# Casting the values of later batches on GpSimd, and loading half of w_in in smaller pieces

## The chip, the cores and the metric

The kernel runs on one core of one Trainium2 chip. The metric is the device time of one execution in microseconds (us); of several runs the median counts. A core has five engines that work side by side, each through its own queue in order: TensorE (PE in the profile, its weight loads PEld), VectorE (DVE), ScalarE (ACT), GpSimd (POOL) and SyncE (SP, which only issues transfers here). They wait for one another, and for transfers, through semaphores.

## What is computed

A linear attention with position-dependent features, and behind it a two-layer network. Per batch and head, for q, k, v of 576 rows and 64 columns:

```python
def phi(x, c, s):                       # c, s: cosine and sine of the row's position
    r = np.maximum(x, 0.0)
    return np.concatenate([r * c, r * s], axis=-1)
q_p, k_p = phi(q, cos_w, sin_w), phi(k, cos_w, sin_w)
kv = np.einsum('bhsf,bhsd->bhfd', k_p, v)
z = np.sum(k_p, axis=2)
num = np.einsum('bhsf,bhfd->bhsd', q_p, kv)
den = np.einsum('bhsf,bhf->bhs', q_p, z)[..., None] + 1e-06
x = num / den                           # 8 batches, 8 heads, then laid out as 4608 x 512
h = x @ w_in                            # 512 x 2048
g = np.maximum(h, 0.0) ** 2
out = g @ w_out                         # 2048 x 512
```

Inputs and output are fp32; the matmuls work on bf16.

## The kernel before

**The work of a batch.** The kernel goes through the 8 batches in turn. The 576 rows of a batch are four main tiles of 128 (j = 0 to 3) and a tail of 64 rows; for the tail, two groups of four heads lie above one another on the 128 partitions. For each batch:
- k, v and q are loaded as fp32 (`declare_load`): one main transfer of 1 MB and two of 64 KB for the tail each. Batch 0 is loaded at the start, batches 1 and 2 from POOL's queue, batches 3 to 7 from SP's queue. There is one buffer for each of k, v, q, so a load waits until the batch before has been read.
- Features (`declare_feature`, helper `relu_scale`, L406 on ACT and L408 on DVE): relu times cosine, relu times sine, to bf16.
- Values (`declare_v`): v is cast to bf16 into the tile vx, with a column of ones beside each head's 64 columns, so that the sums z come out of the same matmul. It has 65 columns a head, five main buffers and two for tails. From batch 3 on, all five casts of a batch are put on ACT (L413, helper `copy`).
- Key-value products (`declare_kz`): matmuls of kp and vx over the five tiles; then the numerators and denominators (`declare_num`), the division on DVE (L637 to L639), and a transpose of x. From batch 2 on the transposes of the query features and of x are DMAs from SP's queue.
- First layer: for batches 0 to 2 plain matmuls (`declare_plain`) with relu on ACT (L416) and square on DVE (L419); from batch 3 on a scheme with seven products instead of eight (`declare_seven1`), with sums of x and of w_in made on DVE (L427, tiles xs and w1s), added to a PSUM bank with relu by L422 on DVE.
- Second layer: `declare_rows` for batch 0, then `declare_pair`, again seven products, with sums of g (tile gs, L427) and results (ysb).

All matmuls of these stages go through the helper `mm`, L430.

**How the order is made.** The functions named `declare_...` don't issue anything. Each adds operations to a `Planner`, with the engines that may do it, an assumed cost, and what it reads and writes. The planner then plays the whole program through with these costs, picks an engine and a place in its queue for each operation, with hand-made shifts of due times (`SHIFTS`), and the kernel issues the operations in that order. So what stands ahead of what on an engine is fixed when the program is built; at run time an engine only waits. In `declare_v` the cost of a cast is 0.52 us on ACT and 0.34 on DVE for a main tile; `declare_att` calls it with ACT alone from batch 3 on.

**How w_in comes in.** `prologue` issues the loads of batch 0 from SP's queue. On POOL's queue it waits for the tail of v (L1090), and then issues w_in in four quarters of columns with `load_w1(i, 4)`, L373. A quarter is 512 columns for 512 rows: 128 partitions with four rows each, read as fp32 and written as bf16 (so the transfer casts). The planner is told of them by four entries that are `GIVEN`, one a quarter, 2.6 us apart. The first layer of batch 0 starts with columns 0 to 255 (blocks hb 0 and 1 of 128), then 256 to 511, and so on. POOL's later transfers (batches 1 and 2, w_out with `load_w2`, the output of batch 0) are in the plan; after some 56 us POOL has nothing more to do.

Of the kernel before, what the change touches and what calls it, by code (L numbers as in the profile page):

```python
# [10 lines left out]
ALU = mybir.AluOpType  # L11
# [40 lines left out]
class Planner:  # L52
# [23 lines left out]
    def add(self, engs, fn, r=(), w=(), pos=None, lat=None, size=None, after=(), land=2.2, held=None, begin=0.0):  # L76
        if isinstance(engs, tuple):
            engs = {engs[0]: engs[1]}
        if size:
            lat = land + size  # L80
        op = Op(engs, fn, pos, lat, size)
        op.land, op.held, op.begin = land, held, begin
        for k in r:
            if k in self.writer:
                op.deps.add(self.writer[k])
            self.readers.setdefault(k, []).append(op)
        for k in w:
            if k in self.writer:
                op.deps.add(self.writer[k])
            op.deps.update(x for x in self.readers.get(k, ()) if x is not op)  # L90
            self.writer[k], self.readers[k] = op, []
        for k in list(r) + list(w):
            b = k[0] if isinstance(k, tuple) else k
            if isinstance(b, Buf) and b not in op.bufs:
                op.bufs.append(b)
                b.users += 1
        op.after = set(after) - op.deps
        op.deps |= op.after
        self.ops.append(op)
        return op  # L100
# [133 lines left out]
def kernel(  # L234
# [9 lines left out]
    nc = tc.nc  # L244
    P = nc.NUM_PARTITIONS
    B, H, S, D = q.shape
# [70 lines left out]
    def at(buf, name=None):  # L317
        return mem[name or buf.pool][:, buf.i]
# [13 lines left out]
    def constants():  # L332
        sidx = const.tile([P, J + 1], F32, name="sidx")
        for p0, p1, c, n, base, mult in [
            (0, P, 0, J, 0, J),
            (0, TAIL, J, 1, MAIN, 1),
            (TAIL, P, J, 1, MAIN, 1),
        ]:
            nc.gpsimd.iota(
                sidx[p0:p1, c : c + n],  # L340
                pattern=[[1, n]],
                base=base,
                channel_multiplier=mult,
                allow_small_or_imprecise_dtypes=True,
            )
        bias_pi2 = const.tile([P, 1], F32, name="bias_pi2")
        nc.vector.memset(bias_pi2, math.pi / 2.0)
        theta_scale = (math.pi / 2.0) / S
        nc.scalar.activation(cos_col, sidx, ACTF.Sin, bias=bias_pi2[:], scale=-theta_scale)
        nc.scalar.activation(sin_col, sidx, ACTF.Sin, bias=0.0, scale=theta_scale)  # L350
        make_identity(nc, ident)
# [3 lines left out]
    def load_main(src, nm, i, b, eng, parts=(slice(None),)):  # L355
        main = mem[nm][:, i]
        for js in parts:
            eng.dma_start(  # L358
                out=main[:, :, js, :],
                in_=src[b, :, 0:MAIN, :].rearrange("h (p j) d -> p h j d", j=J)[:, :, js, :],  # L360
            )

    def load_tail(src, nm, i, b, eng):
        tail = mem[nm + "t"][:, i]
        for g in range(2):
            eng.dma_start(  # L366
                out=tail[g * TAIL : (g + 1) * TAIL, :, :],
                in_=src[b, g * HH : (g + 1) * HH, MAIN:S, :].rearrange("h p d -> p h d"),
            )

    def load_w1(i, n):
        f0, f1 = i * DFF // n, (i + 1) * DFF // n
        nc.gpsimd.dma_start(  # L373
            out=w1sb[:, :, f0:f1],
            in_=moe_w_in[:, f0:f1].rearrange("(kb p) f -> p kb f", p=P),
        )
# [35 lines left out]
    def copy(eng, out, in_):  # L412
        (nc.scalar.copy if eng == "ACT" else nc.vector.tensor_copy)(out=out, in_=in_)  # L413
# [39 lines left out]
    def cached(d, key, pool):  # L453
        if key not in d:
            d[key] = plan.buf(pool)
        return d[key]
# [15 lines left out]
    def source(nm, b, j):  # L472
        return loaded[nm if j < J else nm + "t", b]
# [6 lines left out]
    def piece(nm, b, j):  # L480
        t = at(source(nm, b, j))
        return t[:, :, j, :] if j < J else t
# [35 lines left out]
        add({e: cost[e] for e in engs}, feature, r=[source_key(nm, b, j)], w=[(buf, j % 2, part)])  # L518

    def declare_v(b, j, engs):  # L520
        buf = cached(vxb, (b, j), "vx" if j < J else "vxt")
        n = 1 if j < J else 0.65
        cost = {"ACT": 0.52 * n, "DVE": 0.34 * n}

        def cast(eng):
            copy(eng, at(buf)[:, :, 0:D], piece("v", b, j))

        add({e: cost[e] for e in engs}, cast, r=[source("v", b, j)], w=[buf])

# [501 lines left out]
    def declare_att(b, kpos, npos, cos_k=BOTH, cos_q=DVE1, cast=ACT1):  # L1031
        for j in range(NS):
            declare_feature("k", b, j, "c", cos_k)
            declare_feature("k", b, j, "s", ACT1)
            declare_v(b, j, cast)
        declare_kz(b, kpos)
        for j in range(NS):
            declare_feature("q", b, j, "c", cos_q)
            declare_feature("q", b, j, "s", ACT1)
            if b > 1 and (j == J or j % 2):  # L1040
                declare_qT(b, j // 2)
            elif b == 1:
                declare_qT_pe(b, j, npos[j] - 3.5, DVE1)
        for j in range(NS):
            declare_num(b, j, npos[j])
            if b > 1 and (j == J or j % 2):
                declare_xT(b, j // 2)
            elif b == 1:
                declare_xT_pe(b, j, npos[j] + 2.0, BOTH)
# [19 lines left out]
    def prologue():  # L1069
        for src, nm, part in (  # L1070
            (k, "k", 0), (k, "kt", 0), (q, "q", 0), (v, "vt", 0), (v, "v", 0), (v, "v", 1), (q, "q", 1), (q, "qt", 0)
        ):
            if nm[1:]:
                load_tail(src, nm[0], 0, 0, nc.sync)
            elif nm == "k":
                load_main(src, nm, 0, 0, nc.sync)
            elif nm == "q":
                load_main(src, nm, 0, 0, nc.sync, [slice(part * J // 2, (part + 1) * J // 2)])
            else:
                h = slice(part * HH, (part + 1) * HH)  # L1080
                nc.sync.dma_start(
                    out=mem["v"][:, 0, h],
                    in_=v[0, h, 0:MAIN, :].rearrange("h (p j) d -> p h j d", j=J),
                )
        nc.vector.memset(zeros, 0.0)
        for t in ("vx", "vxt"):
            nc.vector.memset(mem[t][:, :, :, D:E1], 1.0)
        constants()
        fill(28)
        nc.gpsimd.tensor_copy(out=w1sb[0:1, 0, 0:1], in_=mem["vt"][0:1, 0, 0, 0:1])  # L1090
        for i in range(4):
            load_w1(i, 4)

    def fill(n):
        for _ in range(n):
            nc.tensor.matmul(out=banks[:, SPARE, :], lhsT=zeros[:, 0:P], rhs=zeros, start=True, stop=True)
# [11 lines left out]
    def declare_first():  # L1108
# [4 lines left out]
        for j in range(2):  # L1113
            for c in "cs":
                feature("q", j, c)
        declare_v(0, J, BOTH)
        ks = [plan.buf("B"), plan.buf("B")]
        kvzb[0] = plan.buf("kvz")
# [185 lines left out]
    with tc.manual_schedule():  # L1304
        prologue()
        end = None
        for op in plan.plan(t0):
            if op.eng == "PE" and op.start < SPARE_UNTIL:
                if end:
                    fill(int((op.start - end - 0.2) / 0.22))  # L1310
                end = op.end
            op.fn(op.eng)
# [29 lines left out]
```

## Time and profile before

| what | value |
|---|---|
| median of 3 runs | 278.38 us (277.17 to 278.71) |
| the profiled execution | 276.82 us, span of its instructions 274.8 us |
| granted TensorE clock | 1.000 |
| matmuls and weight loads | 2845 each |
| DMA queue of POOL | 12.32 MB, 17.1% of 16 engines' span |
| DMA queue of SP and ACT | 40.12 MB, 58.4% |
| ACT casts of vx from v | 26 main ones, mean 636 ns |
| transfers of w_in | 4, median 10.5 us from issue to landing |

The profile shows one execution. Busy time is the time in which an engine has an instruction in work; matmuls are pipelined, so their durations overlap, and a short stop of PE shows in the distance from one start to the next rather than in its busy time. A group of instructions is given by line, engine, operation, the tiles out<-in, their shapes (partitions x elements, type) and their number; then busy time and the mean of one in ns, then the engine's idle time before them and what ended it. In a timeline each row is a start, a duration, and in brackets the idle time before it with what ended that. The chain of work that ended last is followed back from the last instruction to whatever released it.

### The profile page before, as it was taken

The page shows a single profiled execution, that of the slowest core. Times are in us where ns is not written, and L with a number is a line of the kernel's source. Part 1 is how long each engine was busy: PE and PEld are TensorE (multiplying, and loading weights), DVE is VectorE, ACT ScalarE, POOL GpSimd, SP SyncE. Part 2 cuts the span into 40 slices and gives each one's busy share as a digit, 9 for nine tenths or more (in the row PEclk, how much of TensorE's full clock was granted, in tenths as well). Part 3 has the DMA queues.
Part 4 walks back from the last instruction along what each step waited for, and adds up shares of the span by engine and source line. Part 5 has one row for each costly group of instructions (what it writes and reads, how often), then busy time and mean ns, then how long its engine had stood idle before and what let it go on. Part 6 is the DMA issues. An engine that isn't in the chain of part 4 may idle for free.

```text
span 274.8 us, 7115 instructions
## 1 busy us (share of the span) xinstructions
PE 267.9 (98%) x2845; PEld 227.6 (83%) x2845; DVE 218.9 (80%) x515; ACT 194.9 (71%) x391; POOL 21.6 (8%) x38
## 2 busy tenths in 40 slices
PE   8979999999999999999999999999999999999994
PEld 3668856789988988888888898988988888888884
DVE  1789996997694989699968999799968798279652
ACT  3876982997895598589957994699735954684522
POOL 1453544010000000000000000000000000000000
PEclk9999999999999999999999999999999999999999
DMA  7999999969979998899299955996198301200025
GB/s 217 321 205 290 296 283 365 219 218 225 361 160 186 281 334 156 224 347 221 81 164 308 259 181 102 265 338 217 35 205 170 91 2 44 95 16 2 1 79 153
DMA packets 81840, 53.01 MB, mean 193 GB/s; under 512 B 53584, under 2 KB 77648, under 8 KB 81808
## 3 DMA queue, kind: packets, MB, share of 16 engines
q1 hardware_dynamic: 75136, 40.12, 58.4%
q0 software_dynamic: 6528, 12.32, 17.1%
q8 instruction: 22, 0.36, 0.5%
q10 hardware_dynamic: 144, 0.13, 0.1%
q14 instruction: 10, 0.08, 0.1%
HBM read 36.70 MB, written 9.44 MB: 168 GB/s over the span
## 4 chain that ended last, share of the span: by engine, by line
PE 80%; DMA 8%; DVE 7%; issue 1%; SPq 1%; POOL 1%; ACT 1%; DVEq 0%
PE banks L430 79%; DMA w1sb<-in_moe_w_in_dram 4%; DMA qpT<-qp 2%; DMA vt<-in_v_dram 2%; DVE rs L422 2%; DVE gT L419 2%; DVE gs L427 2%; PE banks L591 1%; DVE x L639 1%; POOL w1sb L373 1%; SPq L366 0%; PE banks L682 0%; DVE qp L408 0%; DVE kp L408 0%; SPq L358 0%
## 5 line engine op out<-in xcount | busy, mean ns | idle before, releaser
L430 PEld LDWEIGHTS <-w1sb 128*128 128x128 bf16 x784 | 73.0, 98 | 10.4 <-DMA w1sb<-in_moe_w_in_dram 1.4
L430 PE MATMUL banks<-xT,w1sb 128*128 128x256 bf16 (+1 forms) x576 | 68.4, 267 | 1.0 <-DMA w1sb<-in_moe_w_in_dram 1.0
L430 PEld LDWEIGHTS <-gs 128*128 128x128 bf16 x512 | 49.0, 98 | 5.9 <-DVE gs L427 0.2
L416 ACT ACTIVATE rt<-banks 128x512 bf16<-128x512 f32 x64 | 37.2, 600 | 14.9 <-PE banks L430 9.3
L430 PEld LDWEIGHTS <-gT 128*128 128x128 bf16 x400 | 38.0, 98 | 9.0
L430 PE MATMUL banks<-w2sb,gT 128*128 128x256 bf16 (+1 forms) x288 | 44.2, 296 | 0.0
L430 PEld LDWEIGHTS <-w1s 128*128 128x128 bf16 x320 | 30.7, 98 | 3.7
L430 PE MATMUL banks<-w2sb,gs 128*128 128x256 bf16 x256 | 33.0, 273 | 0.0
L430 PE MATMUL banks<-w2s,gs 128*128 128x256 bf16 x256 | 32.2, 273 | 0.0
L422 DVE CUSTOM_DVE_ANT_0 rs<-banks,sums 128x512 bf16<-128x512 f32 x40 | 27.0, 684 | 4.5 <-ACT sums L847 3.1
L419 DVE TENSOR_TENSOR gT<-rs 128x1024 bf16<-128x1024 bf16 (+1 forms) x50 | 27.7, 579 | 1.8 <-ACT rs L416 1.0
L416 ACT ACTIVATE rs<-banks 128x512 bf16<-128x512 f32 x40 | 23.6, 604 | 3.1 <-PE banks L430 2.9
L430 PE MATMUL banks<-xs,w1s 128*128 128x256 bf16 x160 | 23.0, 273 | 0.0
L430 PE MATMUL banks<-xT,w1s 128*128 128x256 bf16 x160 | 22.9, 273 | 0.0
L419 DVE TENSOR_TENSOR gT<-rt 128x512 bf16<-128x512 bf16 x48 | 19.2, 418 | 4.5 <-ACT rt L416 4.3
L427 DVE TENSOR_TENSOR ysb<-banks,sums 128x256 f32<-128x256 f32 x32 | 13.4, 418 | 11.2 <-PE banks L430 7.3
L406 ACT ACTIVATE qp<-q,sin_col 128x512 bf16<-128x512 f32 x31 | 22.1, 738 | 0.1
L639 DVE TENSOR_TENSOR x<-banks,den 128x512 bf16<-128x512 f32 x30 | 20.7, 691 | 1.0
L406 ACT ACTIVATE kp<-k,sin_col 128x512 bf16<-128x512 f32 x30 | 21.2, 734 | 0.0
L427 DVE TENSOR_TENSOR gs<-gT 128x1024 bf16<-128x1024 bf16 x28 | 19.2, 686 | 1.1 <-PE banks L430 0.7
L413 ACT CAST vx<-v 128x512 bf16<-128x512 f32 x26 | 16.2, 636 | 0.9 <-DMA v<-in_v_dram 0.9
L637 DVE TENSOR_SCALAR den<-banks 128x8 f32<-128x8 f32 (+1 forms) x38 | 6.0, 159 | 12.5 <-PE banks L430 12.3
(106 smaller groups left out, 364.0 us busy)
## 6 DMA issues: line engine op xcount, KB each, us to landing
out_dram<-ysb SPq DMA_DIRECT2D x13, 512.0 KB, 3.5
k<-in_k_dram SPq DMA_DIRECT2D x6, 1024.0 KB, 6.4
v<-in_v_dram SPq DMA_DIRECT2D x5, 1024.0 KB, 7.9
q<-in_q_dram SPq DMA_DIRECT2D x5, 1024.0 KB, 9.3
w1sb<-in_moe_w_in_dram POOLq DMA_DIRECT2D x4, 512.0 KB, 10.5
q<-in_q_dram POOLq DMA_DIRECT2D x2, 1024.0 KB, 11.2
w2sb<-in_moe_w_out_dram POOLq DMA_DIRECT2D x4, 512.0 KB, 11.6
k<-in_k_dram POOLq DMA_DIRECT2D x2, 1024.0 KB, 11.3
```

The lines of the kernel that those rows point to most:

```text
L373: nc.gpsimd.dma_start(out=w1sb[:, :, f0:f1], in_=moe_w_in[:, f0:f1].rearrange("(kb p) f -> p kb f", p=P),)
L406: nc.scalar.activation(out=dst, in_=src, func=ACTF.Relu, scale=col)
L413: (nc.scalar.copy if eng == "ACT" else nc.vector.tensor_copy)(out=out, in_=in_)
L416: nc.scalar.activation(out=out, in_=in_, func=ACTF.Relu)
L419: nc.vector.tensor_tensor(out=out, in0=in_, in1=in_, op=ALU.mult)
L422: nc.vector._custom_dve(TENSOR_ADD_SAT, out=out, in0=in0, in1=in1, s0=float("inf"), s1=0.0)
L427: nc.vector.tensor_tensor(out=out, in0=in0, in1=in1, op=op)
L430: nc.tensor.matmul(out=out, lhsT=lhsT, rhs=rhs, start=start, stop=stop, skip_group_check=True)
L591: nc.tensor.transpose(t[:, h, :], qp_at(b, j)[:, h, :], ident[:, :])
L637: nc.vector.tensor_single_scalar(out=d, in_=n4[:, :, :, D], scalar=EPS, op=ALU.add)
L639: nc.vector.tensor_tensor(out=x_at(b, j).rearrange("p (b k) (l d) -> p b k l d", b=n, l=2), in0=n4[:, :, :, 0:D].rearrange("p b (k l) d -> ...
```

## The change

Two things. In the prologue, the first two quarters of w_in are loaded in two pieces each, so that there are six transfers on POOL's queue, in the order of the columns: four of 256 columns, then two of 512. In `declare_v`, the cast of a batch from 3 on is issued as a GpSimd instruction, whatever engine the planner chose for it. It reads the same piece of v and writes the same part of vx, and multiplies by 1.0 twice. That is 25 instructions: five batches with four main tiles and a tail. The planner isn't told: in its account these casts still take ACT's time, so the order on the other engines is the one of before, with the casts left out of ACT's queue and put, in the same order, on POOL's.

```diff
     def declare_v(b, j, engs):
+
         buf = cached(vxb, (b, j), "vx" if j < J else "vxt")
         n = 1 if j < J else 0.65
         cost = {"ACT": 0.52 * n, "DVE": 0.34 * n}
 
         def cast(eng):
-            copy(eng, at(buf)[:, :, 0:D], piece("v", b, j))
+            if b > 2:
+                nc.gpsimd.tensor_scalar(
+                    out=at(buf)[:, :, 0:D], in0=piece("v", b, j), scalar1=1.0, scalar2=1.0, op0=ALU.mult, op1=ALU.mult
+                )
+            else:
+                copy(eng, at(buf)[:, :, 0:D], piece("v", b, j))
...
         nc.gpsimd.tensor_copy(out=w1sb[0:1, 0, 0:1], in_=mem["vt"][0:1, 0, 0, 0:1])
         for i in range(4):
+            load_w1(i, 8)
+        for i in range(2, 4):
             load_w1(i, 4)
```

## The prediction

> **What bounds the kernel now.** I read the page's totals first, then the waits of TensorE, then the queue around each line that the change touches. The totals of the page:
>
> ```profile
> PE 267.9 (98%) x2845; PEld 227.6 (83%) x2845; DVE 218.9 (80%) x515; ACT 194.9 (71%) x391; POOL 21.6 (8%) x38
> ```
>
> TensorE (PE) works 267.9 of 274.8 us. So almost nothing can be won behind it: a change that shortens ACT pays only where PE waits for ACT. These are all waits of PE at its main line L430 that the waits view lists:
>
> ```profile
> PE banks L430 <- DMA w1sb<-in_moe_w_in_dram: 1.0, 2, 0.9
> PE banks L430 <- ACT sums L847: 0.3, 1, 0.3
> PE banks L430 <- DMA qpT<-qp: 0.2, 1, 0.2
> ```
>
> Counted from start to start of neighbouring matmuls they are a little longer: 1.03 and 0.32 us for two quarters of w_in (at 18.6 and 21.8 us), 0.51 us at 123.1 (ACT), 0.36 us at 142.8 (the transposed queries). That is 2.2 us in all, the most that a perfect change of these parts could give. The first two, in PE's timeline (start, duration, then what it waited for):
>
> ```profile
> 17.72 1.06 PE L430 MATMUL banks<-xT,w1sb 128*128 128x128 bf16 x16
> 19.64 1.05 PE L430 MATMUL banks<-xT,w1sb 128*128 128x256 bf16 x8 [0.86 <-DMA w1sb<-in_moe_w_in_dram]
> 20.77 1.03 PE L430 MATMUL banks<-xT,w1sb 128*128 128x256 bf16 x8
> 22.19 1.05 PE L430 MATMUL banks<-xT,w1sb 128*128 128x256 bf16 x8 [0.16 <-DMA w1sb<-in_moe_w_in_dram]
> ```
>
> VectorE (DVE) is not slack either. The chain that ended last leaves PE at 113.8 us, stays on DVE nearly all the way to 137.4, and comes back through one DMA:
>
> ```profile
> 137.36 0.02 issue
> 137.39 5.83 DMA qpT<-qp
> 143.22 0.05 issue
> 143.26 128.08 PE banks L430 x1304
> ```
>
> PE waited only 0.36 us there, so PE and DVE arrive together: whatever makes DVE later between 113 and 136 us makes PE later.
>
> The moved instructions, from the view of the tile vx after 60 us:
>
> ```profile
> L413 ACT CAST vx<-v x20: 610/632/681, 74.6 to 191.8; 128x512 bf16<-128x512 f32 x20
> ```
>
> They are 20 main casts, and the groups show 5 tails of 413 ns: 12.6 + 2.1 = 14.7 us of ACT. Nobody is listed as waiting for them. What GpSimd (POOL) takes for arithmetic shows only in tiny rows, by form:
>
> ```profile
> masks.py:199 POOL TENSOR_SCALAR_AFFINE_SELECT ident<-ident 128x128 bf16<-128x128 bf16 x1 | 0.3, 292 | 0.1
> L1090 POOL CAST w1sb<-vt 1x1 bf16<-1x1 f32 x1 | 0.2, 177 | 6.8 <-DMA vt<-in_v_dram 6.8
> ```
>
> [...] At 28.45 to 29.33 POOL issued a transfer:
>
> ```profile
> 28.51 0.42 DVE L427 TENSOR_TENSOR w1s<-w1sb 128x512 bf16<-128x512 bf16 x1
> 28.85 0.72 DVE L408 TENSOR_SCALAR qp<-q,cos_col 128x512 bf16<-128x512 f32 x1
> 29.49 0.41 DVE L419 TENSOR_TENSOR gT<-rt 128x512 bf16<-128x512 bf16 x1
> ```
>
> The feature instruction in it took 0.72 us where this line takes 0.48 undisturbed; another at 16.65 (a tail) took 0.69 where 0.35 is usual. The two-input ones kept their 0.42. No GpSimd instruction that reads SBUF for long stands in this trace[...]. [...]
>
> **w_in in pieces.** Taken away: two transfers of 512 KB; added: four of 256 KB. POOL then issues six instead of four, at 0.78 us each: the last is issued at 13.9 instead of 12.3 us. Nothing on POOL waits behind that, since its next transfer (q of batch 1) starts at 16.35, held by DVE. POOL's transfers take eight semaphores in turn, and each waits for the landing of the eighth before it; after the last two quarters all that follow are pushed by the same two, so k of batch 1 still waits for the third quarter and nothing new is late. SP's queue is untouched.
>
> When do the bytes land? The quarters land at 16.34, 19.59, 22.14 and 24.74 us: from the second on, one per 2.57 us, with GpSimd's packets back to back on all 16 DMA engines. The queue of transfers is the limit, not the moment of issue. So the third quarter can't come earlier because the first two are cut; it can come later, if smaller packets cost more. A quarter is 512 packets of 1024 B, 32 per engine, 80 ns each. SP's packets took 46 ns at 1024 B and 27 ns at 512 B, so some 8 ns of a packet are fixed (2 x 27 - 46). A half packet then takes (80 - 8) / 2 + 8 = 44 ns, a piece 32 x 44 = 1.41 us, two pieces 2.82: 0.25 us more per cut quarter, 0.5 for both. Bounds: 0, if no part is fixed; 5.1 us if a half packet costs a whole one, which the 27 ns speak against; I keep 0 to 1 us for the range.
>
> Where does the stall go? PE stops at 18.56 for the second quarter. Its first piece would land at about 18.0, so that this stop goes; the second lands at 20.1 and holds PE from 19.7 to 20.1; after 1.1 us of work it stands before the third quarter, which lands at 22.64 instead of 22.14. PE resumes at 22.7, not 22.2. The stall is paid once, at its end: **+0.5 us**.
>
> **Casts off ACT.** The 14.7 us come off an engine that PE waits for once, 0.51 us at 123.1: there a cast of 0.62 us stands ahead of the copy L847 which PE needs. That wait goes; but at 131 PE then waits for DVE (below), so I count 0. If DVE isn't held, it is a gain of 0.5.
>
> **Casts on POOL.** Cost of one: extrapolating the two rows, (292 - 177) / 128 ns an element gives 0.177 + 512 x 0.0009 = 0.64 us[...]. I take 0.8 for a main cast and 0.45 for a tail[...]. They start when v has landed, since POOL has nothing else: at 72.5, 98.6, 122.1, 155.8 and 182.0 us by the trace's landings. POOL ends a batch's casts some 4 to 6 us later. The key-value matmuls that read them start at 86.3, 102.2, 129.9, 160.5 and 198.6, later groups of a batch later still; two casts of batch 6 are done at 157.6. So PE doesn't wait for the casts themselves, and SP's next load of v, which waits for them, gets its buffer earlier than before.
>
> **What they do to DVE** is the cost. [...] PSUM sources (L422, L639, L427 ysb) run on. I walk each batch. The one of batch 6:
>
> ```profile
> 154.69 1.27 DVE L408 TENSOR_SCALAR kp<-k,cos_col 128x512 bf16<-128x512 f32 x3
> 155.87 1.28 DVE L422 CUSTOM_DVE_ANT_0 rs<-banks,sums 128x512 bf16<-128x512 f32 x2
> 157.07 0.68 DVE L419 TENSOR_TENSOR gT<-rs 128x1024 bf16<-128x1024 bf16 x1
> 157.67 0.68 DVE L422 CUSTOM_DVE_ANT_0 rs<-banks,sums 128x512 bf16<-128x512 f32 x1
> 158.27 1.01 DVE L419 TENSOR_TENSOR gT<-rs 128x1024 bf16<-128x1024 bf16 x2
> 161.58 0.69 DVE L427 TENSOR_TENSOR gs<-gT 128x1024 bf16<-128x1024 bf16 x1
> 162.30 0.69 DVE L427 TENSOR_TENSOR gs<-gs,gT 128x1024 bf16<-128x1024 bf16 x1
> ```
>
> Cast 1 runs 155.96 to 156.76 under the two L422; cast 2 to 157.56 holds the square of 157.07 by 0.5; cast 3 (158.24 to 159.04) holds the next by 0.3; cast 4 slips in between two squares and costs 0.8. DVE is 1.6 us late and has no gap until the sums gs, which PE uses from 163.05 on, at most 0.65 us after they are ready (I take 0.3). PE stops for 1.3. In the same way:
> - Batch 3: sources are PSUM, PE's stop is 0.
> - Batch 4 (98.6 to 104.7): 0.2 + 0.9 on two squares, 0.4 absorbed by a gap; 0.65 + 0.4 on two later ones, 0.1 absorbed. Late by 1.65; the sums xs end at 109.57 and PE wants them at 110.10. Stop 1.15.
> - Batch 5 (122.1 to 127.6): 0.9 on a feature instruction, of which the gap of 0.47 before 123.71 takes most of 0.55; then 0.1 + 0.8 + 0.8 on squares. Late by 2.0, less 0.2 at the sums for 131.35. Stop 1.8.
> - Batch 7 (182.1 to 187): 0.9 + 0.4 + 0.8 + 0.1 less gaps of 0.25. Late by 1.9, less 0.45 at 190.7. Stop 1.45.
>
> Late in all 7.15 us, slack 1.45, PE stopped **5.7 us**. With w_in: 5.7 + 0.5 = 6.2. The profiled execution took 276.82 us; 276.82 + 6.2 = 283.0. The median of the runs, 278.38, lies 1.56 above the profiled execution, so as a median **284.6 us**. Ends: casts of 0.64 us and w_in 0: 7.15 x 0.8 - 1.45 = 4.3, so 282.7. [...]
>
> **Rivals.** (a) [...] POOL, not DVE, does the waiting, or two-input instructions pass it as those at 28.5 and 29.5 did. DVE's squares come back to back, which speaks for it; the 0.72 us against. Then w_in +0.5 and ACT -0.5 to 0: 276.8 to 277.3, as a median 278.4 to 278.9. (b) [...] 7.15 x 1.6 - 1.45 + 0.5 = 10.5 us: 288.9. For it: POOL's rows here are too small to exclude it[...]. (c) **Faster**: the pieces let all of w_in land at least 0.9 us earlier, because transfers of different pieces overlap better at the start, where the first packet moved only at 12.2 us, 3.1 us after its issue; both stops on w_in go (1.35) and[...] the one on ACT (0.5): 276.82 - 1.85 = 275.0, as a median 276.5. It decides from the third quarter landing before 21.2 us. The steady 2.57 us per quarter speak against it.
>
> **Numbers.** Forecast 0.56, (a) 0.20, (b) 0.17, (c) 0.07. About 0.5% (1.4 us) is what a measurement of this kernel can tell from no change. Faster is (c), 0.07; same is (a), 0.20; slower the rest, 0.73. The range takes in (a) and reaches to (b): 278.0 to 289.0; it leaves out (c) and half of (b). The forecast's own range is 282.7 to 286.5.
>
> **What would show it.** Right: POOL casts of about 0.8 us in five bursts after v's landings; squares and features beside them longer, or with waits before them; new PE stops near 110, 131, 163 and 191 us, each 1 to 2 us; ACT 14.7 us less busy; the third quarter of w_in landing 0.5 us later, PE's wait before it 1.4 us. Wrong: DVE's durations unchanged in the bursts, or stops of PE at the key-value matmuls, which would mean that the casts themselves come late.

## The result and the profile after

The changed kernel takes 279.42 us (median of 12 runs, 278.49 to 280.71), the kernel before in the same measurement 277.68 us (276.55 to 279.61, 12 runs). The ratio is 1.0052, with a 95% interval of 1.0027 to 1.0077: slower by some 1.4 us, where 6.2 were forecast. Measured once more with the experiments, the changed kernel gave 1.0072 (1.0049 to 1.0094), some 2.0 us. Ratios leave out the few executions that were slow at a lower granted TensorE clock (one of the pieces alone took 396.47 us at 0.657). The profiled execution took 279.15 us, with a span of 277.4 us (before: 276.82 and 274.8).

The totals first:

```profile
PE 268.6 (97%) x2845; PEld 227.3 (82%) x2845; DVE 222.8 (80%) x515; ACT 185.9 (67%) x366; POOL 40.1 (14%) x65
```

ACT lost 9.0 us of busy time and not the 14.7 of the casts' durations: instructions on ACT overlap in the profile (before, their durations add up to 223.8 us and the busy time is 194.9). POOL gained 18.5 us, and DVE gained 3.9 without having been given a single instruction: it does the same work and is occupied longer. The waits of PE at L430:

```profile
PE banks L430 <- DVE rs L422: 1.1, 2, 0.8
PE banks L430 <- DMA w1sb<-in_moe_w_in_dram: 1.0, 1, 1.0
PE banks L430 <- ACT vx L413: 0.8, 1, 0.8
PE banks L430 <- DMA qpT<-qp: 0.4, 1, 0.4
PE banks L430 <- DVE gs L427: 0.2, 1, 0.2
```

The wait for ACT's sums L847 is gone. New are the first sums L422 and the sums gs, both of DVE, so PE is now stopped by DVE where before it was stopped by ACT. The wait for vx at L413 lies in batch 0 (12.5 us), where nothing was changed. The kernel with the casts twice (below), whose start is that of before, shows 0.9 us there as well, the other traces at most 0.3. Now w_in, in PE's timeline:

```profile
20.61 1.03 PE L430 MATMUL banks<-xT,w1sb 128*128 128x256 bf16 x8
21.48 0.39 PE L688 MATMUL banks<-ident,x 128*128 128x128 bf16 x4
22.85 1.05 PE L430 MATMUL banks<-xT,w1sb 128*128 128x256 bf16 x8 [0.98 <-DMA w1sb<-in_moe_w_in_dram]
```

The stop before the second quarter is gone, and one stop of 1.14 us stands before the third. That is the picture that the prediction gave: one stall, before the third quarter. The transfers landed at 16.25, 17.57, 18.91, 20.28, 22.80 and 25.34 us. From landing to landing, two pieces took 2.66 to 2.71 us and a whole quarter 2.52 to 2.54.

The chain of work that ended last left DVE for good at 137.4 us before, and does so at 188.6 now. It is no longer brought to PE by the transposed queries alone:

```profile
129.88 0.61 DVE rs L422
130.53 8.14 PE banks L430 x93
138.67 5.82 DMA qpT<-qp
144.54 9.13 PE banks L430 x104
```

At 130.5 PE takes over straight from a sum on DVE, which the chain of before did not show. The casts themselves, from the view of the tile vx and from POOL's timeline:

```profile
L528 POOL TENSOR_SCALAR vx<-v x20: 612/622/1054, 73.2 to 186.7; 128x512 bf16<-128x512 f32 x20
```

```profile
99.38 1.48 POOL L528 TENSOR_SCALAR vx<-v 128x512 bf16<-128x512 f32 x2 [20.20 <-DVE den L644]
...
124.13 2.22 POOL L528 TENSOR_SCALAR vx<-v 128x512 bf16<-128x512 f32 x3
...
157.68 2.80 POOL L528 TENSOR_SCALAR vx<-v 128x512 bf16<-128x512 f32 x4 [10.88 <-DMA v<-in_v_dram]
184.60 3.12 POOL L528 TENSOR_SCALAR vx<-v 128x512 bf16<-128x512 f32 x4 [24.12 <-DMA v<-in_v_dram]
```

The median of a cast is 622 ns, its mean 762 (14.8 us of POOL's busy time for 20), and the longest 1054: some casts ran through, others stood for up to 0.43 us. So both sides waited, POOL for DVE as well as DVE for POOL. DVE beside the burst of batch 6, the stretch that the prediction walked through:

```profile
157.14 1.28 DVE L422 CUSTOM_DVE_ANT_0 rs<-banks,sums 128x512 bf16<-128x512 f32 x2
158.34 1.08 DVE L419 TENSOR_TENSOR gT<-rs 128x1024 bf16<-128x1024 bf16 x1
159.34 0.68 DVE L422 CUSTOM_DVE_ANT_0 rs<-banks,sums 128x512 bf16<-128x512 f32 x1
159.94 1.41 DVE L419 TENSOR_TENSOR gT<-rs 128x1024 bf16<-128x1024 bf16 x2
161.28 0.34 DVE L408 TENSOR_SCALAR kpt<-kt,cos_col 128x256 bf16<-128x256 f32 x1
```

Before, the first square took 0.68 and the pair 1.01. Now they take 1.08 and 1.41, 0.40 more each time. The sums L422, with their PSUM source, took 1.28 and 0.68 as before, although casts ran beside them.

**Where the 2.5 us lie.** PE works in the same order in both kernels, so that the start of each matmul can be set against the same matmul of before. Until the third quarter of w_in (22.19 before, 22.85 after) the changed kernel lost 0.66 us; from there to the last matmul it lost 1.88. The steps of this second part are:

| place (us, before) | step (us) | what PE waits for |
|---|---|---|
| 99.0 | -0.19 | nothing; the kernel before, run again, shows the same step |
| 107.1 | +0.05 | |
| 123.7 and 124.2 | -0.51, -0.05 | ACT's sums L847, no longer |
| 129.5 and 131.4 | +1.00, +0.12 | DVE L422, DVE gs |
| 143.3 | +0.17 | transposed queries |
| 160.5 and 163.1 | +0.43, +0.35 | DVE L422, DVE gs |
| 186.4 | +0.21 | DVE L422 |
| 194 to 196 | +0.13, +0.18 | DVE gs |

They add up to 1.89. DVE's instructions, set against the same ones of before in the same way, show ten that are longer by 0.19 to 0.47 us and none else: 1.13 us in batch 4, 1.24 in batch 5, 0.80 in batch 6, 0.55 in batch 7, together **3.7 us**. All ten read SBUF only (squares L419, features L408), and all lie beside casts.

### The profile page after: what moved, and what is told of

It reads as the page before. It is cut to its first block, busy times and chain, and to the rows that moved or that the text cites. A ratio compares the mean times of both kernels' runs of the same rounds, so it can differ in the third digit from the quotient of the medians.

```text
span 277.4 us, 7143 instructions
## 1 busy us (share of the span) xinstructions
PE 268.6 (97%) x2845; PEld 227.3 (82%) x2845; DVE 222.8 (80%) x515; ACT 185.9 (67%) x366; POOL 40.1 (14%) x65
## 4 chain that ended last, share of the span: by engine, by line
PE 77%; DVE 10%; DMA 8%; issue 1%; POOL 1%; SPq 1%; ACT 0%; ACTq 0%
PE banks L430 76%; DMA w1sb<-in_moe_w_in_dram 4%; DVE rs L422 3%; DVE gT L419 3%; DMA qpT<-qp 2%; DMA vt<-in_v_dram 2%; DVE kp L408 1%; POOL w1sb L373 1%; PE banks L597 1%; DVE gs L427 1%; DVE x L645 1%; PE banks L688 1%; SPq L366 0%; SPq L358 0%; DVE den L644 0%
## 5 line engine op out<-in xcount | busy, mean ns | idle before, releaser
L430 PEld LDWEIGHTS <-w1sb 128*128 128x128 bf16 x784 | 73.0, 98 | 9.6 <-DMA w1sb<-in_moe_w_in_dram 1.1
L430 PE MATMUL banks<-xT,w1sb 128*128 128x256 bf16 (+1 forms) x576 | 68.2, 267 | 1.0 <-DMA w1sb<-in_moe_w_in_dram 1.0
L430 PEld LDWEIGHTS <-gs 128*128 128x128 bf16 x512 | 48.7, 98 | 7.0 <-DVE gs L427 1.0
L430 PEld LDWEIGHTS <-gT 128*128 128x128 bf16 x400 | 38.0, 98 | 9.0
L430 PE MATMUL banks<-w2sb,gT 128*128 128x256 bf16 (+1 forms) x288 | 44.2, 296 | 0.0
L430 PEld LDWEIGHTS <-w1s 128*128 128x128 bf16 x320 | 30.7, 98 | 4.6 <-issue 1.0
L430 PE MATMUL banks<-w2sb,gs 128*128 128x256 bf16 x256 | 33.0, 273 | 0.0
L430 PE MATMUL banks<-w2s,gs 128*128 128x256 bf16 x256 | 32.3, 273 | 0.2 <-DVE gs L427 0.2
L419 DVE TENSOR_TENSOR gT<-rs 128x1024 bf16<-128x1024 bf16 (+1 forms) x50 | 29.6, 616 | 1.8 <-ACT rs L416 1.0
L422 DVE CUSTOM_DVE_ANT_0 rs<-banks,sums 128x512 bf16<-128x512 f32 x40 | 26.9, 683 | 4.2 <-ACT sums L853 2.8
L528 POOL TENSOR_SCALAR vx<-v 128x512 bf16<-128x512 f32 x20 | 14.8, 762 | 89.1 <-DMA v<-in_v_dram 52.5
L430 PE MATMUL banks<-xT,w1s 128*128 128x256 bf16 x160 | 22.9, 273 | 0.8 <-DVE rs L422 0.8
L419 DVE TENSOR_TENSOR gT<-rt 128x512 bf16<-128x512 bf16 x48 | 19.6, 427 | 4.4 <-ACT rt L416 4.2
L430 PE MATMUL banks<-xs,w1s 128*128 128x256 bf16 x160 | 23.0, 273 | 0.0
L427 DVE TENSOR_TENSOR ysb<-banks,sums 128x256 f32<-128x256 f32 x32 | 13.4, 418 | 11.0 <-PE banks L430 7.2
L645 DVE TENSOR_TENSOR x<-banks,den 128x512 bf16<-128x512 f32 x30 | 20.7, 691 | 1.0
L427 DVE TENSOR_TENSOR gs<-gT 128x1024 bf16<-128x1024 bf16 x28 | 19.3, 688 | 1.1 <-PE banks L430 0.7
L430 PE MATMUL banks<-xTt,w1sb 128*128 128x256 bf16 x128 | 15.8, 273 | 0.0
```

Source lines behind the costliest of these rows:

```text
L419: nc.vector.tensor_tensor(out=out, in0=in_, in1=in_, op=ALU.mult)
L422: nc.vector._custom_dve(TENSOR_ADD_SAT, out=out, in0=in0, in1=in1, s0=float("inf"), s1=0.0)
L427: nc.vector.tensor_tensor(out=out, in0=in0, in1=in1, op=op)
L430: nc.tensor.matmul(out=out, lhsT=lhsT, rhs=rhs, start=start, stop=stop, skip_group_check=True)
L528: nc.gpsimd.tensor_scalar(out=at(buf)[:, :, 0:D], in0=piece("v", b, j), scalar1=1.0, scalar2=1.0, op0=ALU.mult, op1=ALU.mult)
L645: nc.vector.tensor_tensor(out=x_at(b, j).rearrange("p (b k) (l d) -> p b k l d", b=n, l=2), in0=n4[:, :, :, 0:D].rearrange("p b (k l) d -> ...
```

## The experiments

Theory: POOL's casts hold DVE's SBUF instructions, and what PE loses is that lateness less what DVE has in hand; ACT's relief is worth the 0.5 us at 123 us; the pieces of w_in cost some tenths at most. First rival: the pieces and the start cost the time, not the casts. Second rival: the casts come late for their readers, or the new order on POOL and ACT matters, whether the casts hold DVE or not.

All ratios are against the kernel before in the same measurement, with a 95% interval. As a measure of what such a ratio can tell, the kernel before was also built and run once more as if it were a new one.

**The same kernel again**, without an edit.

> The kernel before, unchanged, measured against itself. Both theories: ratio 1.000 within 0.002. It shows how far the start differs from one execution to the next: in the executions so far with whole quarters the third quarter of w_in landed at 22.14, 22.8, 21.86 and 23.1 us; here again somewhere from 21.8 to 23.2.

Measured: 278.65 us against 277.46, ratio 1.0029 (1.0007 to 1.0051). So one build differs from another of the same kernel by 0.3%, more than the 0.2% expected, and outside of its own interval. Ratios within 0.3% of 1 are therefore not read as effects below. The trace tells more: from the third quarter of w_in to the last matmul this build took 248.95 us, the first profile of the kernel before 248.87. What scatters most is the start. PE went on with the third quarter at 23.18 us in this execution and at 22.19 in the other.

**The casts alone**, w_in in four quarters.

```diff
-            copy(eng, at(buf)[:, :, 0:D], piece("v", b, j))
+            if b > 2:
+                nc.gpsimd.tensor_scalar(...)
+            else:
+                copy(eng, at(buf)[:, :, 0:D], piece("v", b, j))
```

> The casts on GpSimd alone, w_in in four quarters as before. Theory A (GpSimd's casts hold VectorE[...], and TensorE stops for what VectorE makes later): in the trace of the changed kernel TensorE lost 1.8 of its 2.54 us after the w_in stage, so this kernel loses 1.8 us, ratio about 1.0065, with about ten VectorE instructions longer by 0.35 to 0.45 us beside the casts, and TensorE stops near 130, 162 and 165 us. Theory B (the pieces of w_in and the late start are the whole loss, the casts cost nothing and give back the wait on ScalarE at 123 us): 0 to -0.5 us, ratio 0.998 to 1.000.

Measured: 279.49 us, ratio 1.0061 (1.0034 to 1.0088). Ten DVE instructions longer, by 3.5 us in all; PE's steps at the same places and of the same sizes as in the full change (-0.51 at 123, +0.98 at 130, +0.21 and +0.35 near 162, +0.15 at 186). The casts alone bring all of the loss that can be told from scatter.

**The pieces alone**, casts on ACT.

```diff
         for i in range(4):
+            load_w1(i, 8)
+        for i in range(2, 4):
             load_w1(i, 4)
```

> The pieces of w_in alone, casts on ScalarE as before. Theory A (the transfers' rate is the limit, the stop moves to the third quarter): third quarter lands 0.5 to 0.7 us later than the 22.14 us of before, TensorE stops once for 1.1 to 1.4 us before it, loss 0.5 to 0.7 us, ratio about 1.002. Theory B (the pieces are the whole loss): 1.4 to 1.8 us, ratio 1.005 to 1.0065. A third case: the later landing of the second half of v of batch 0 (12.76 instead of 11.65 us in the changed kernel) belongs to the one execution and not to the pieces; then it is absent here, and TensorE's end of this stage is the same all the same, as the third quarter decides.

Measured: 278.76 us, ratio 1.0045 (1.0025 to 1.0064); of this run only the times are used. To get a trace it was built and run once more:

> The pieces of w_in alone once more, for a trace at full clock. Theory A (half packets cost a little more, the stop is paid at the third quarter): pieces land 1.33 us apart, a cut quarter takes 2.66 to 2.71 instead of 2.55 us, so 0.25 to 0.3 us for two, ratio 1.001 to 1.002. Theory B (something in the pieces costs the 1.0045 of the first measurement): 1.0 to 1.5 us, and TensorE must then show it in the stage up to 25 us as a start later by about that much, since nothing later was changed.

Measured: 278.57 us, ratio 1.0018 (0.9990 to 1.0045). The first ratio lies above the 0.3% by which a kernel differs from itself, the second below it, so the two can't tell a cost of the pieces from none. The start of the first layer in this execution, and then in the repeated kernel before, in PE's timeline:

```profile
19.83 1.04 PE L430 MATMUL banks<-xT,w1sb 128*128 128x256 bf16 x8
20.70 0.39 PE L683 MATMUL banks<-ident,x 128*128 128x128 bf16 x4
22.25 1.05 PE L430 MATMUL banks<-xT,w1sb 128*128 128x256 bf16 x8 [1.17 <-DMA w1sb<-in_moe_w_in_dram]
```

```profile
20.64 1.05 PE L430 MATMUL banks<-xT,w1sb 128*128 128x256 bf16 x8 [1.21 <-DMA w1sb<-in_moe_w_in_dram]
...
23.18 1.05 PE L430 MATMUL banks<-xT,w1sb 128*128 128x256 bf16 x8 [0.15 <-DMA w1sb<-in_moe_w_in_dram]
```

With pieces PE starts the second quarter without a wait and stands before the third; with quarters here it is the other way round. The third quarter has the last word in both. Over all traces of the same order, PE goes on with it at 22.19, 23.18, 22.85, 21.90, 23.14, 22.29, 22.58 and 22.59 us with quarters (mean 22.59) and at 22.85, 22.25 and 22.31 with pieces (mean 22.47). An effect of the pieces is below this scatter.

**No casts.** The casts of batches 3 to 7 are left out.

```diff
+            if b > 2:
+                pass
+            else:
                 copy(eng, at(buf)[:, :, 0:D], piece("v", b, j))
```

> This kernel leaves out the casts of the values of batches 3 to 7 altogether; w_in in quarters as before. It shows what ScalarE's relief of 14.7 us is worth with no cast on GpSimd. Theory A: the 0.5 us stop of TensorE at 123 us goes, the rest is hidden: -0.4 to -0.7 us, ratio about 0.998. Against it: if ScalarE paced TensorE at more places than the waits show, -1.5 us or more, ratio 0.995 or less.

Measured: 276.98 us, ratio 0.9986 (0.9969 to 1.0003). No DVE instruction is longer. The stop at 123 us goes (-0.51), and then PE waits 0.15 more for the queries at 143 and 0.37 more near 151, there for ACT. From the third quarter on it takes 248.84 us, against 248.87. So with this order, freeing ACT of the casts, and without any cost elsewhere, is worth nothing that can be measured.

**The casts twice** on POOL, the second one a repetition of the first.

```diff
+                nc.gpsimd.tensor_scalar(...)
+                nc.gpsimd.tensor_scalar(...)
```

> Each cast on GpSimd is issued twice, the second writing the same values to the same place; w_in in quarters as before. Theory A: twice the GpSimd time beside VectorE, so about 20 held VectorE instructions and 7 to 8 us of lengthening instead of 3.7; TensorE loses about twice what it lost to the casts plus the slack that is now used up: 4 to 5.5 us, ratio 1.014 to 1.020. If instead GpSimd only gets through where VectorE lets it: the same 1.8 us, ratio about 1.0065. If the casts' own lateness counted, TensorE would stop at the key-value matmuls that read vx.

Measured: 284.33 us, ratio 1.0230 (1.0199 to 1.0260), a little above the 1.014 to 1.020 expected. 24 DVE instructions are longer, 7.9 us in all. In batch 6, DVE's timeline:

```profile
162.58 0.71 DVE L408 TENSOR_SCALAR kpt<-kt,cos_col 128x256 bf16<-128x256 f32 x1
163.21 0.67 DVE L422 CUSTOM_DVE_ANT_0 rs<-banks,sums 128x512 bf16<-128x512 f32 x1
163.92 2.57 DVE L419 TENSOR_TENSOR gT<-rs 128x512 bf16<-128x512 bf16 x3
```

Three squares in a row that took 1.36 us take 2.57, which is 0.40 each; the feature of a tail takes 0.71 instead of 0.34; the L422 between them takes its usual 0.67. The waits of PE at L430 follow:

```profile
PE banks L430 <- DVE gs L427: 1.9, 4, 0.9
PE banks L430 <- DVE rs L422: 1.1, 1, 1.1
PE banks L430 <- ACT vx L413: 0.9, 1, 0.9
PE banks L430 <- DVE gT L419: 0.8, 1, 0.8
```

Three of these four are for DVE, and the one for vx is that of batch 0 again. No stop is for a cast on POOL.

**Write only.** POOL copies one element of v, so that it waits for the same transfer, and then fills vx with a constant. The values are left out; POOL writes as much as before and reads next to nothing.

```diff
+                nc.gpsimd.tensor_copy(out=at(buf)[0:1, 0, 0:1], in_=piece("v", b, j)[0:1, 0, 0:1])
+                nc.gpsimd.memset(at(buf)[:, :, 0:D], 0.001)
```

> This kernel puts a constant in the place of the values of batches 3 to 7: in the place of each cast GpSimd copies one element of v (so that it starts when v has landed) and then sets the whole tile to a constant, which writes but reads nothing; w_in in quarters. If[...] two-input instructions of VectorE are held only beside a GpSimd instruction that reads: squares and sums keep their 0.42 and 0.68 us, only features (L408) are longer by about 0.36, and TensorE loses less than with the casts: ratio 0.999 to 1.003. If any GpSimd instruction holds any VectorE instruction with two SBUF inputs: as with the casts, ratio about 1.006.

Measured: 276.95 us, ratio 0.9975 (0.9954 to 0.9996), just below the 0.999 expected and within the 0.3%. DVE and POOL in batch 6:

```profile
156.43 0.68 DVE L419 TENSOR_TENSOR gT<-rs 128x1024 bf16<-128x1024 bf16 x1
157.03 0.68 DVE L422 CUSTOM_DVE_ANT_0 rs<-banks,sums 128x512 bf16<-128x512 f32 x1
157.63 1.01 DVE L419 TENSOR_TENSOR gT<-rs 128x1024 bf16<-128x1024 bf16 x2
```

```profile
156.11 0.53 POOL L529 MEMSET vx<- 128x512 bf16 x1
156.58 0.57 POOL L528 CAST vx<-v 1x1 bf16<-1x1 f32 x1
157.21 0.53 POOL L529 MEMSET vx<- 128x512 bf16 x1
157.67 1.01 POOL L528 CAST vx<-v 1x1 bf16<-1x1 f32 x1
158.74 0.63 POOL L529 MEMSET vx<- 128x512 bf16 x1
```

The squares take 0.68 and 1.01 as before the change. The fill at 156.11 ends in the first square's time, and the one at 157.21 in the next square's, and neither is felt. The copies of one element, which read, take 0.57 and 1.01 here where they take 0.18 alone: it was POOL that waited. Only two feature instructions are longer, by 0.35 each: beside features a fill took 0.76 instead of 0.53, and the feature behind it, where one followed, was held. So in these runs it takes POOL's reading to hold the squares (0.40 us each beside the casts, 0 beside the fills); that POOL works and writes is not enough. Whether reading alone would do, without the writing, no run shows.

**Half of each cast**: four of eight heads on a main tile, two of four on a tail; the rest is left out.

```diff
+                n4 = 4 if j < J else 2
+                nc.gpsimd.tensor_scalar(
+                    out=at(buf)[:, 0:n4, 0:D], in0=piece("v", b, j)[:, 0:n4], ...
```

> The casts on GpSimd take only half of the heads (256 instead of 512 elements a partition; the other half is left out); w_in in quarters. Theory A: a held instruction waits for what is left of a cast. A cast of 256 elements takes 0.41 instead of 0.62 us, so a hold shrinks from 0.36 to 0.41 to about 0.15 to 0.2 us; lengthening in all from 3.5 to about 1.7 us, ratio 1.001 to 1.003. If a hold is a fixed price of changing over, the lengthening stays above 3 us and the ratio near 1.006.

Measured: 277.76 us, ratio 1.0003 (0.9986 to 1.0021). A half cast takes 0.40 us undisturbed. Seven DVE instructions are longer, by 0.11 to 0.25 us, 1.23 us in all. In batch 6:

```profile
158.00 0.79 DVE L419 TENSOR_TENSOR gT<-rs 128x1024 bf16<-128x1024 bf16 x1
158.71 0.68 DVE L422 CUSTOM_DVE_ANT_0 rs<-banks,sums 128x512 bf16<-128x512 f32 x1
159.31 1.01 DVE L419 TENSOR_TENSOR gT<-rs 128x1024 bf16<-128x1024 bf16 x2
```

0.11 on one square, nothing on the pair. The cast's duration fell to 0.64 of a whole one, the lengthening of DVE's instructions to a third.

**Only batch 5 on POOL.**

```diff
-            if b > 2:
+            if b == 5:
```

> Only the casts of batch 5 on POOL, w_in in quarters, the order as it was. Theory (each POOL burst costs the time by which it makes DVE late, less what DVE has in hand): the wait at 123 us goes (-0.5), DVE is held two or three times, about 1.2 us, and TensorE stops for the first sum L422 near 130 us by about 0.9 more than before; from the third quarter of w_in to the last matmul 0.5 to 0.9 us longer than before, ratio 1.002 to 1.003. Rival (bursts add up differently: a stop at 130 is given back at the later stops of batches 6 and 7, which are not there now): 0 to 0.3 us, ratio 1.000 to 1.001.

Measured: 277.67 us, ratio 1.0009 (0.9989 to 1.0030). PE and DVE around 123 and 130 us:

```profile
122.57 1.04 PE L430 MATMUL banks<-xTt,w1sb 128*128 128x256 bf16 x8
123.44 0.60 PE L430 MATMUL banks<-xs,w1sb 128*128 128x256 bf16 x4
...
129.81 0.60 PE L430 MATMUL banks<-xT,w1s 128*128 128x256 bf16 x4 [0.54 <-DVE rs L422]
```

```profile
124.31 2.46 DVE L419 TENSOR_TENSOR gT<-rs 128x1024 bf16<-128x1024 bf16 x3
```

The wait at 123 is gone, as it is in every trace in which batch 5's casts have left ACT. Three DVE instructions are longer by 0.94 us in all (the three squares 2.46, before 1.88), and PE stops for 0.54 at 129.8. From the third quarter on: 249.05 us, 0.18 more than before. The size is the rival's (0 to 0.3), not the theory's (0.5 to 0.9): the burst fell 0.3 us better for DVE than in the full change, and PE's steps were -0.51 at 123, +0.70 and +0.13 at 130, +0.17 at 143. What was gained at ACT is paid back 6 us later, to DVE.

**The casts planned.** The planner gets the casts of batches from 3 on as operations of POOL.

```diff
-        cost = {"ACT": 0.52 * n, "DVE": 0.34 * n}
+        cost = {"ACT": 0.52 * n, "DVE": 0.34 * n, "POOL": 0.65 * n}
...
-        add({e: cost[e] for e in engs}, cast, r=[source("v", b, j)], w=[buf])
+        add({e: cost[e] for e in (("POOL",) if b > 2 else engs)}, cast, r=[source("v", b, j)], w=[buf])
```

> The casts from batch 3 on are given to POOL in the plan, with a cost of 0.65 us (0.42 for a tail), w_in in quarters; so the order on all engines is made anew with ACT free of them. Theory: [...] DVE is held about ten times by 0.4 us as in the changed kernel, and the freed time of ACT is worth at most the 0.4 us that leaving the casts out was worth; ratio 1.002 to 1.008. Rival (what was lost was only the order: with ACT's free time known, work goes from DVE to ACT, and DVE's holds are covered): ratio 0.993 to 0.999.

Measured: 283.79 us, ratio 1.0203 (1.0160 to 1.0245), which is outside both expectations. The waits of PE at L430:

```profile
PE banks L430 <- DVE rs L422: 1.7, 4, 0.7
...
PE banks L430 <- DMA w1sb<-in_moe_w_in_dram: 1.1, 3, 0.5
PE banks L430 <- DVE x L645: 0.6, 1, 0.6
PE banks L430 <- ACT sums L973: 0.5, 1, 0.5
```

Only five DVE instructions are longer than their form usually is, 1.8 us in all, half of the full change. So most of the 5.6 us must come with the other order, in which PE stops in many places for sums, divisions and copies that each come some tenths late. Which entries of the order do it was not followed up; the shifts of due times were made for the order of before. So this plan doesn't mend the change; whether another would is open.

**The changed kernel again.**

> The changed kernel once more, to see how far one kernel differs between builds and executions. Theory: from the third quarter of w_in to the last matmul 250.6 to 250.9 us as in its first profile and in the kernel with the casts alone (250.75 and 250.55); ratio 1.004 to 1.008. Rival (what was read off one execution is scatter): a value nearer to the 248.9 us of the kernel before.

Measured: 279.20 us, ratio 1.0072 (1.0049 to 1.0094); ten DVE instructions longer, 3.5 us; from the third quarter on 250.94 us, just above the 250.6 to 250.9 expected.

All traces side by side, from PE's start on the third quarter of w_in to its last start, with the lengthening of DVE's instructions:

| kernel | DVE longer (us) | third quarter to last matmul (us) | against before |
|---|---|---|---|
| before, and again | 0, 0 | 248.87, 248.95 | 0, +0.08 |
| pieces alone | 0 | 248.31 | -0.56 |
| no casts | 0 | 248.84 | -0.03 |
| write only | 0.7 | 248.71 | -0.16 |
| batch 5 only | 0.9 | 249.05 | +0.18 |
| half casts | 1.2 | 249.54 | +0.67 |
| casts alone | 3.5 | 250.56 | +1.69 |
| changed, and again | 3.7, 3.5 | 250.75, 250.94 | +1.88, +2.07 |
| casts twice | 7.9 | 254.63 | +5.76 |

With PE's order kept, 3.5 to 3.7 us of lengthening cost 1.7 to 2.1 us, and 7.9 us cost 5.8. Of the smaller lengthenings the table shows no clear effect, since a single wait for a transfer weighs as much. Three such waits stand in it. In the half casts +0.89 is a stop at 120.6 for sums on ACT, which had stood 1.13 us for a landing of k: without it the row would be -0.22. In the write-only kernel, and in the changed one again, +0.58 is a wait for transposed queries at 175.9. And in the pieces alone the -0.56 is the stop at 123, which is gone although the casts are on ACT. ACT's timelines there, of the kernel before, of the same again, and of the pieces alone:

```profile
122.09 0.62 ACT L413 CAST vx<-v 128x512 bf16<-128x512 f32 x1 [0.86 <-DMA v<-in_v_dram]
```

```profile
123.20 0.62 ACT L413 CAST vx<-v 128x512 bf16<-128x512 f32 x1 [1.15 <-DMA v<-in_v_dram]
```

```profile
121.40 0.62 ACT L413 CAST vx<-v 128x512 bf16<-128x512 f32 x1 [0.24 <-DMA v<-in_v_dram]
```

ACT stands at the cast until v has landed, and the copy L847 stands behind it. PE then stops for 0.51, 0.81 and 0 us. So this stop is made by the landing of v as much as by the cast, and what the relief of ACT takes away differs from one execution to the next.

## Why the prediction was right in kind and wrong in size

Slower was right, and so was the cause: not one stop of PE is for a cast, the stops are for DVE, and DVE is late because ten of its SBUF instructions wait beside POOL's casts, by 0.19 to 0.47 us each. The size forecast was 6.2 us and the result 1.4 to 2.0. Step by step:

- **"w_in in pieces ... +0.5 us".** Where the stall goes was right: the second quarter's stop vanished, the third quarter's took its place, 1.14 us long (1.4 foretold). The cost of a cut quarter was 0.12 to 0.19 us, a little over half of the 0.25 named. Pairs of pieces in other executions took up to 3.4 us, and whole second quarters up to 3.6, so these sizes are those of one trace. From their spacing in it, 42 ns at 512 B and 79 at 1024 B on each of the 16 engines, an estimate of the fixed part of a packet is 5 ns (2 x 42 - 79), not the 8 that SP's packets gave. In the end the start scatters by more than a microsecond, and the term can't be seen: that PE came to the third quarter 0.66 us later in this trace agrees with the +0.5 by luck. That k of batch 1 still waits for the third quarter, the eighth of POOL's transfers before it with pieces as with quarters, was right: 1.31 us before, 0.99 now.
- **"Casts off ACT ... I count 0".** The stop of 0.5 us at 123 did go, in every kernel that moved batch 5's casts. But the prediction laid it to the 0.62 us of the cast alone; ACT had stood 0.86 us for v before it, and the stop was 0 to 0.81 us in the traces with the cast on ACT. The 0 held in a sense that was not meant: with no casts at all the gain is given back at 143 and 151 us, and the step of +0.17 at 143 in the full change, which the kernel without casts shows as +0.15, belongs to this too.
- **"A cast on POOL: I take 0.8".** Undisturbed it takes 0.62, next to the 0.64 that two small rows of the trace gave; a tail takes 0.41, where 0.45 was taken. The 0.8 was the author's estimate, and no trace of before showed it.
- **"Late in all 7.15 us, slack 1.45, PE stopped 5.7 us".** This is the step that failed, and in it the size of DVE's holds. Before the gaps were taken off, the walk through the batches had 15 holds with a sum of 8.55 us, 0.57 each. The trace shows 10 holds with a sum of 3.7, 0.37 each: two thirds of the holds, and two thirds of their size. By batch, in us:

| batch | holds foretold | measured | PE's stops foretold | measured |
|---|---|---|---|---|
| 4 | 2.15 | 1.13 | 1.15 | 0.05 |
| 5 | 2.6 | 1.24 | 1.8 | 1.12 |
| 6 | 1.6 | 0.80 | 1.3 | 0.78 |
| 7 | 2.2 | 0.55 | 1.45 | 0.52 |
| all | 8.55 | 3.7 | 5.7 | 2.5 |

Two thirds of the lengthening were to reach PE, and two thirds did; that the share came out so well is partly luck, since in batch 4 nearly all was absorbed (in the second trace of the changed kernel 0.44 us reached PE there). From the 2.5 us goes what ACT's relief gave.

Why smaller: that a cast holds the next SBUF instruction until it ends, for all that is left of 0.8 us, was the author's assumption, which the trace of before did not show. No hold is longer than 0.47 us, while a cast is in work for 0.62; in the walk seven holds are 0.8 or 0.9. A half cast takes 0.40 and holds for up to 0.25. So 256 elements cost 0.22 us of the cast, and 512 cost 0.44, which is about the longest hold in both; the other 0.18 is what a one-element copy takes in all. The casts that had to wait show the same: over all traces they end 0.47 to 0.48 us after the instruction of DVE that they stood behind, casts of 256 elements 0.26 to 0.27 after it, and one-element copies 0.04. By an estimate from these durations, the 0.18 us of a cast before its elements pass are over by then, and a hold is the part in which elements pass, some 0.86 ns each ((0.62 - 0.40) / 256).

Why fewer: casts and squares do alternate, in the walk as in the trace, but a cast that has stood behind a square is done 0.48 us after it, where the walk gave it 0.8. In the burst of batch 6 the walk's third cast outlasts the L422 beside it and holds the next square by 0.3, and its fourth costs 0.8. In the trace the cast behind the first square (158.85 to 159.90) is done before the L422 that ends at 160.02, and costs nothing. Three holds were foretold (0.5, 0.3, 0.8), and there were two of 0.40. A waiting cast doesn't always get in behind one square: a one-element copy of 1.01 us and, with the casts twice, a cast of 1.45 us stood through two squares in a row.

The trace of before left two points open, and the runs answer them. Two-input squares are held beside a GpSimd instruction that reads SBUF: six in the changed kernel, by 0.19 to 0.47 us, and four features L408 by 0.35 to 0.36. The squares are not held beside one that only writes (0 in the write-only kernel). And instructions with a PSUM source run free: seven L422, three divisions (L645 now, L639 before) and one sum ysb (L427), each with casts beside it for 0.41 to 0.75 us, are within 0.02 us of their durations before. In batch 3, where 0 was foretold because of these sources, no instruction is longer by over 0.05 us (a sum gs, which reads SBUF only, by just that). A hold for a whole cast, as in the walk, is too long for the measured holds by the 0.18 us above.

The rivals: (a), that POOL does the waiting or DVE's instructions pass, was nearer in time (278.4 to 278.9, measured 279.4) than the forecast, but not in cause, since ten instructions of DVE are held, for 3.7 us. (b), a cast 1.6 times as long as the 0.8 taken, is refuted by the 622 ns, and (c) by the landing of the third quarter at 22.80, far from the 21.2 it needed.

## What to carry to other kernels

Work that is moved to GpSimd is not free of VectorE: here 25 casts of 0.62 us (0.41 for a tail) made ten VectorE instructions longer, by 0.47 us at most. So count the SBUF-only instructions of VectorE beside such work, and give each meeting one wait of the streaming part of one instruction (0.44 us for these casts by the estimate above), on both sides, rather than every GpSimd instruction a full hold. Before moving work off an engine, ask what its absence is worth; here leaving the casts out altogether changed the time by no more than can be measured (0.9986, interval to 1.0003), so with this order no placement of them could have gained. An instruction that waits for a transfer at the head of an engine's queue holds all that stands behind it: at 123 us in the kernel before, ACT stood 0.86 us for v, and PE 0.51 for the copy behind the cast. And cutting a transfer in pieces can move a wait on to the next transfer: here the queue set the landings (in the profiled execution a quarter in 2.5 to 2.7 us, cut or whole), and the 1.03 us before the second quarter became 1.14 before the third.

## What was not expected of the hardware

- A GpSimd fill of 128x512 bf16, 0.53 us, did not hold two-input VectorE instructions at all, and one-input features twice, by 0.35 us.
- A one-element copy on GpSimd took 0.18 us alone, and up to 1.01 beside squares: this tiny read waited 0.83 us, as long as the cast of 1.45 us did in the kernel with the casts twice.
- A packet of GpSimd's casting transfers lasts 60 ns at 512 B and 98 at 1024, but the packets follow one another on an engine after 42 and 79 ns by the landings: they overlap, so their durations are no price. The cut quarter took 0.12 to 0.19 us more.
- The start of the kernel differs from execution to execution by up to 1.3 us at the third quarter of w_in (21.90 to 23.18). The rest repeats to some tenths, but for single waits on transfers, which moved it by up to 0.9 us.
